# Batch 0's softmax denominators in two halves, output stores on SyncE's queue, and a re-planned order of work, in an attention-plus-feed-forward kernel

## The chip, the cores and the metric

One NeuronCore of a Trainium2 chip runs the whole kernel. The metric is device time in microseconds (us) of one execution; less is better. The kernel before was timed four times.

## What is computed

Inputs are q, k and v (8 batches, 8 heads, 576 positions, head size 64), `moe_w_in` (512 x 2048) and `moe_w_out` (2048 x 512), all float32. The reference, cut to what matters:

```python
q_d, k_d, v_d = means over groups of 4 neighbouring positions      # 144 of them
out_d  = softmax(q_d @ k_d.T / 8) @ v_d                            # coarse attention, 144 x 144
out_up = np.repeat(out_d, 4, axis=2)
s      = q @ k.T / 8, masked to |i - j| < 4
out_local = softmax(s) @ v                                         # a band of 7
x = (out_up + out_local), heads side by side                       # 4608 tokens x 512
h = x @ w_in
g = np.where(h > 0, h, exp(min(h, 0)) - 1)
out = g @ w_out                                                    # 4608 x 512
```

## The kernel before, in words

Heads are worked on in pairs: four pairs for each batch. The tokens of all batches stand in one row and are cut into nine blocks of 512 for the feed-forward part, so block 0 needs only batch 0, and block 1 needs batches 0 and 1.

All five engines work from one list, the string `ORDER`. A loop at the end of the kernel takes its words one by one and emits the instructions of each. Every engine executes its own instructions strictly in the order of the list and waits only for its operands and for its buffers, so the list is the schedule. The words, with b the batch, j the pair, t the token block and fc one of 16 slices of the hidden layer:

- `Lq Lk Lv b.j` load q, k or v of a pair by SyncE's queue (SP; lines 306 and 316), into ten staging buffers. `Dq Dk b.h` load two pairs of q or k at once, converted to 16 bits on the way, by GpSimd's queue (POOL; line 336). `WI0`-`WI3` and `WO0`-`WO3` load the weights, also by POOL (lines 266, 271). `WL` holds a staging buffer for a load.
- `Cq Ck Cv` convert to 16 bits on POOL (lines 354, 359).
- `Tq Tk` turn q and k by TensorE (PE), `Aq Ak` copy them out of PSUM (mostly ScalarE, ACT), `Fq Fk` sum fours on VectorE (DVE).
- `SL` and `SD` are the local and the coarse scores of a pair (PE), and `SC` is both together. `G0 G1` and `H0 H1` are their exponentials on ACT (lines 502, 508), and `E0 E1` are both together. `M` applies the mask on DVE.
- `VS` sums v in fours by PE (line 369), `VD` copies the sum out (DVE).
- `DEN` sums the exponentials of all four pairs of a batch into denominators (PE, line 539, 96 small matmuls), `RC` takes the reciprocal (DVE), `RB` spreads it to 128 rows (PE, line 573).
- `OUT` is probabilities times v (PE, lines 584 and 590), `LG` copies it out (ACT, lines 599 and 602), `MUL` multiplies by the reciprocals (DVE), `X b.j.t` adds the local and the coarse part into block t (mostly POOL, line 627).
- `mm1.t.fc` is a slice of x @ w_in (4 matmuls, PE, line 635); for block 0, `Q0`-`Q2` do the first three quarters of slices 0 to 3. `e`, `m` and `g` are the exponential (ACT, line 660), the minimum (DVE, line 664) and the sum (DVE, line 669) of the activation. `mm2.t.i` is a quarter of a 128-token row block of g @ w_out (4 matmuls, PE, line 679). `oc` copies the result out of PSUM (ACT, line 686), and `st` stores it (line 690).
- `Z1`-`Z3` put that many dummy matmuls ("busy", line 251) ahead of the next PE step that takes a fresh PSUM buffer of kind `two` or `more`.

PSUM buffers: `two` (2 buffers) for turns, v sums, outputs, spreads and later scores; `more` (2 buffers) for batch 0's scores, its denominators, its last v sum and the first two spreads. When `Q0` comes up, the room of `more` is handed to `hp` and `misc`, which hold the slices of mm1, the results of mm2 and later denominators.

A DMA on SP's or ACT's queue counts its landing on one of eight semaphores that both queues share. In the built program each of these DMAs waits for an earlier one that used its semaphore to land. The wait stands on the engine that issues the DMA. The stores are issued by ACT:

```python
def store(t, tt):                                      # L688
    r = TBLK * t + 128 * tt
    nc.scalar.dma_start(out=out[r : r + 128, :], in_=oss.pop((t, tt))[:])
```

and the denominators are one step:

```python
den = dens[b] = more("den")[:, 0, :] if b == 0 else bank("misc", "den")
...
                    for j in range(NPAIR):
...
                        nc.tensor.matmul(
                            den[32 * j : 32 * j + 32, 0:RG], lhsT, rhs,
...
                            tile_position=(0, 32 * j),
```

Of the kernel before, what the change touches and what calls it, by code (L numbers as in the profile page):

```python
# [27 lines left out]
NPAIR = H // 2  # L28
# [8 lines left out]
X_DVE, K_DVE = ((0, 3, 0),), ((0, 0), (0, 1))  # L37
ORDER = """
KM Lq0.0 KV TBL Lk0.0 FILL Lq0.1 KN Lk0.1 KE Lq0.2 KI Lk0.2 Cq0.0 Ck0.0 Lq0.3 Tq0.0 Lk0.3 Aq0.0
Tk0.0 Cq0.1 Lv0.0 Ak0.0 Ck0.1 Lv0.1 Z1 Tq0.1 Fq0.0 Lv0.2 SL0.0 Cq0.2 Aq0.1 Lv0.3 Fk0.0 Ck0.2  # L40
Tk0.1 G00.0 Z1 Tq0.2 Ak0.1 Cq0.3 G10.0 Fq0.1 Aq0.2 SD0.0 Ck0.3 Tk0.2 H00.0 Fk0.1 H10.0 KS Ak0.2
M0.0 SL0.1 Z2 Tq0.3 G00.1 Fq0.2 Cv0.0 G10.1 Fk0.2 Aq0.3 SD0.1 M0.1 Tk0.3 H00.1 H10.1 Fq0.3 Cv0.1
Ak0.3 SL0.2 Z1 VS0.0 Dq1.0 Fk0.3 G00.2 G10.2 VD0.0 WI0 SD0.2 WI1 Z2 VS0.1 H00.2 H10.2 Cv0.2
SL0.3 VD0.1 M0.2 G00.3 Z3 VS0.2 G10.3 Dk1.0 M0.3 SD0.3 OUT0.0 H00.3 VD0.2 WI2 H10.3 LG0.0 Z1
DEN0 WI3 WLv1.0 OUT0.1 Cv0.3 Lv1.0 RC0 Lv1.1 LG0.1 Lv1.2 VS0.3 RB0.0 Lv1.3 VD0.3 MUL0.0 RB0.1 Z1
OUT0.2 MUL0.1 X0.0.0 OUT0.3 LG0.2 X0.0.1 LG0.3 RB0.2 X0.1.1 X0.1.0 MUL0.2 Z1 RB0.3 Q0 MUL0.3
X0.2.1 X0.2.0 Q1 X0.3.0 Dk1.1 Q2 Dq1.1 mm1.0.0 mm1.0.2 e.0.0 X0.3.1 Tq1.1 WO0 Tk1.1 e.0.2 m.0.0
mm1.0.1 g.0.0 Ak1.1 WO1 mm1.0.3 Aq1.1 m.0.2 mm1.0.6 Fk1.1 WO2 e.0.3 Fq1.1 e.0.1 Tq1.0 Dk2.0
Tk1.0 Aq1.0 m.0.3 m.0.1 Ak1.0 g.0.1 WO3 SC1.1 Fq1.0 WLv2.0 Dq2.0 Lv2.0 mm1.0.7 Fk1.0 E01.1 Lv2.1
Cv1.0 Lv2.2 g.0.3 E11.1 Lv2.3 g.0.2 VS1.0 Lq3.0 mm1.0.11 VD1.0 e.0.7 M1.1 mm1.0.13 e.0.6 m.0.7  # L50
e.0.11 g.0.7 SC1.0 m.0.6 e.0.13 mm1.0.5 m.0.11 g.0.11 E01.0 m.0.13 mm1.0.9 E11.0 g.0.13 g.0.6
Tq1.2 Tk1.2 M1.0 Aq1.2 mm1.0.14 Ak1.2 Lk3.0 Cv1.1 Fq1.2 OUT1.0 e.0.5 Fk1.2 mm1.0.4 e.0.9 m.0.5
LG1.0 g.0.5 Tq1.3 e.0.4 Dq2.1 m.0.9 VS1.1 g.0.9 Aq1.3 mm2.0.0 VD1.1 e.0.14 Fq1.3 Tk1.3 OUT1.1
Ak1.3 Dk2.1 m.0.4 g.0.4 LG1.1 Fk1.3 SC1.2 m.0.14 g.0.14 mm2.0.1 E01.2 mm1.0.12 E11.2 mm1.0.8
e.0.12 M1.2 SC1.3 Lv3.0 m.0.12 e.0.8 g.0.12 Cv1.2 E01.3 m.0.8 mm1.0.10 g.0.8 E11.3 VS1.2 e.0.10
mm1.0.15 M1.3 VD1.2 DEN1 e.0.15 m.0.10 g.0.10 OUT1.2 m.0.15 mm2.0.2 RC1 LG1.2 g.0.15 RB1.1 RB1.0
MUL1.1 mm2.0.3 MUL1.0 X1.1.1 RB1.2 oc.0.0 MUL1.2 X1.0.2 mm2.0.4 X1.1.2 X1.0.1 Tq2.1 st.0.0 Tk2.1
Aq2.1 Cv1.3 mm2.0.5 Ak2.1 Fq2.1 X1.2.1 VS1.3 Fk2.1 Tq2.2 X1.2.2 mm2.0.6 Aq2.2 VD1.3 OUT1.3 Fq2.2
RB1.3 LG1.3 mm2.0.7 MUL1.3 Tk2.2 oc.0.1 mm2.0.8 Cv2.0 Lq3.1 Ak2.2 mm2.0.9 X1.3.2 Fk2.2 X1.3.1
mm2.0.10 st.0.1 Cv2.1 mm2.0.11 VS2.0 oc.0.2 mm2.0.12 Cv2.2 Lk3.1 VD2.0 SC2.1 mm2.0.13 E02.1  # L60
mm2.0.14 E12.1 Cv2.3 Lv3.1 mm2.0.15 M2.1 Tq2.0 oc.0.3 Cq3.0 Lq3.2 Tk2.0 Aq2.0 mm1.1.0 Ak2.0
Fq2.0 mm1.1.2 e.1.0 Ck3.0 Lk3.2 Fk2.0 SC2.2 e.1.2 m.1.0 g.1.0 E02.2 m.1.2 mm1.1.4 Lv3.2 g.1.2
Cv3.0 E12.2 Lq3.3 Tq2.3 e.1.4 M2.2 mm1.1.1 Aq2.3 Lk3.3 m.1.4 VS2.3 st.0.3 g.1.4 Cq3.1 Tk2.3
e.1.1 VD2.3 mm1.1.3 Ak2.3 m.1.1 Lv3.3 g.1.1 Ck3.1 SC2.0 e.1.3 Fk2.3 mm1.1.7 E02.0 m.1.3 g.1.3
E12.0 VS2.2 Fq2.3 Cv3.1 Lq4.0 mm1.1.5 e.1.7 VD2.2 M2.0 SC2.3 e.1.5 m.1.7 mm2.1.0 Lk4.0 E02.3
g.1.7 m.1.5 E12.3 mm1.1.6 g.1.5 Lv4.0 VS2.1 M2.3 e.1.6 mm1.1.8 VD2.1 m.1.6 DEN2 e.1.8 g.1.6
Cv3.2 Lq4.1 OUT2.1 RC2 mm1.1.9 LG2.1 m.1.8 g.1.8 RB2.1 st.0.2 OUT2.3 e.1.9 MUL2.1 mm1.1.10 LG2.3
m.1.9 RB2.3 g.1.9 X2.1.3 e.1.10 OUT2.0 X2.1.2 MUL2.3 mm1.1.11 LG2.0 m.1.10 RB2.0 g.1.10 X2.3.2
e.1.11 mm2.1.1 MUL2.0 Cv3.3 mm1.1.12 m.1.11 g.1.11 X2.0.3 OUT2.2 e.1.12 X2.0.2 RB2.2 LG2.2
mm1.1.14 m.1.12 g.1.12 X2.3.3 Tq3.0 e.1.14 MUL2.2 mm1.1.13 Aq3.0 Cq3.2 Tk3.0 m.1.14 e.1.13 Lk4.1  # L70
mm2.1.2 VD3.0 X2.2.2 Ak3.0 g.1.14 Tq3.2 Ck3.2 KD3.0 mm1.1.15 m.1.13 Aq3.2 Lv4.1 g.1.13 Cv4.0
Lq4.2 Tk3.2 e.1.15 VD3.2 X2.2.3 mm1.2.0 Ak3.2 m.1.15 g.1.15 Tq3.1 e.2.0 KD3.2 mm2.1.3 Aq3.1
Cq3.3 Tk3.1 m.2.0 oc.1.0 Lk4.2 mm1.2.2 VD3.1 Cq4.1 Ak3.1 g.2.0 Ck4.0 mm2.1.4 st.1.0 KD3.1 e.2.2
Ck3.3 SC3.1 mm1.2.12 m.2.2 E03.1 Lv4.2 g.2.2 Cv4.1 Lq4.3 mm2.1.5 E13.1 mm1.2.1 e.2.12 M3.1 SC3.0
m.2.12 e.2.1 g.2.12 mm2.1.6 E03.0 m.2.1 g.2.1 mm1.2.10 E13.0 Cv4.2 Tq3.3 e.2.10 Tk3.3 M3.0 Aq3.3
mm1.2.15 m.2.10 Ak3.3 g.2.10 Cq4.0 mm2.1.7 e.2.15 VD3.3 Lk4.3 KD3.3 mm2.1.8 m.2.15 oc.1.1 Lv4.3
g.2.15 st.1.1 SC3.3 Lq5.0 Lk5.0 mm2.1.9 E03.3 mm2.1.10 E13.3 mm1.2.5 M3.3 SC3.2 e.2.5 mm1.2.6
E03.2 m.2.5 g.2.5 mm2.1.11 E13.2 Tq4.0 e.2.6 M3.2 oc.1.2 Tk4.0 m.2.6 mm2.1.12 st.1.2 g.2.6 Ck4.2
Ak4.0 DEN3 Aq4.0 Ck4.1 KD4.0 mm2.1.13 VD4.0 Lv5.0 RC3 Lq5.1 mm2.1.14 SO3 mm2.1.15 Tq4.1 oc.1.3
Tk4.1 st.1.3 Cq4.2 mm1.2.3 Aq4.1 Cq5.0 Ak4.1 Lk5.1 mm1.2.7 VD4.1 Lv5.1 e.2.3 KD4.1 Tq4.2 Lq5.2  # L80
e.2.7 m.2.3 g.2.3 Tk4.2 SI3 Cq4.3 mm2.2.0 m.2.7 g.2.7 Ck4.3 Aq4.2 Lk5.2 mm1.2.9 Ak4.2 Ck5.0
VD4.2 Lv5.2 mm1.2.4 e.2.9 KD4.2 m.2.9 SC4.2 e.2.4 g.2.9 E04.2 m.2.4 mm1.2.11 g.2.4 E14.2
mm1.2.13 e.2.11 M4.2 SC4.1 e.2.13 m.2.11 mm2.2.1 g.2.11 E04.1 m.2.13 mm1.2.8 E14.1 g.2.13
mm1.2.14 e.2.8 M4.1 m.2.8 SC4.0 e.2.14 g.2.8 E04.0 m.2.14 mm2.2.2 g.2.14 E14.0 OUT3.0 mm2.2.3
MUL3.0 Cv4.3 OUT3.1 oc.2.0 M4.0 Lq5.3 OUT3.3 st.2.0 Lk5.3 MUL3.1 X3.0.3 mm2.2.4 Lv5.3 X3.0.4
MUL3.3 mm2.2.5 X3.1.3 mm2.2.6 X3.3.4 X3.1.4 OUT3.2 X3.3.3 Tq4.3 MUL3.2 Cv5.1 mm2.2.7 Aq4.3
X3.2.3 Tk4.3 VD4.3 oc.2.1 mm2.2.8 Ck5.2 Ak4.3 mm1.3.0 st.2.1 X3.2.4 KD4.3 Cv5.0 SC4.3 e.3.0
mm1.3.3 Cv5.2 E04.3 Lq6.0 m.3.0 mm2.2.9 E14.3 g.3.0 Tq5.0 e.3.3 M4.3 mm1.3.7 Aq5.0 m.3.3 g.3.3
Cq5.1 DEN4 e.3.7 VD5.0 Cq5.3 Lk6.0 mm1.3.6 RC4 m.3.7 Tk5.0 SO4 g.3.7 Tq5.1 e.3.6 Ck5.1 Ak5.0
mm1.3.5 m.3.6 Aq5.1 Lv6.0 g.3.6 Cq5.2 mm2.2.10 Lq6.1 e.3.5 KD5.0 VD5.1 Lk6.1 mm1.3.1 m.3.5 Lv6.1  # L90
g.3.5 Lq6.2 Tk5.1 e.3.1 mm1.3.8 Lk6.2 Ak5.1 m.3.1 g.3.1 mm2.2.11 SI4 KD5.1 mm1.3.11 e.3.8 SC5.1
oc.2.2 m.3.8 g.3.8 e.3.11 mm2.2.12 E05.1 m.3.11 g.3.11 mm1.3.10 E15.1 mm1.3.9 e.3.10 M5.1 st.2.2
SC5.0 m.3.10 e.3.9 mm2.2.13 g.3.10 E05.0 m.3.9 mm1.3.13 g.3.9 E15.0 mm1.3.4 e.3.13 M5.0 Tq5.2
m.3.13 e.3.4 g.3.13 Tk5.2 Aq5.2 mm2.2.14 m.3.4 g.3.4 Ck5.3 Ak5.2 mm1.3.2 VD5.2 Ck6.0 Lv6.2 KD5.2
mm2.2.15 e.3.2 m.3.2 OUT4.2 oc.2.3 g.3.2 OUT4.0 st.2.3 MUL4.2 mm1.3.14 Cv5.3 mm2.3.0 MUL4.0
e.3.14 X4.2.4 Lq6.3 X4.2.5 OUT4.1 OUT4.3 m.3.14 MUL4.1 X4.0.5 mm2.3.1 X4.0.4 MUL4.3 mm1.3.12
X4.1.5 g.3.14 Tq5.3 e.3.12 X4.3.4 Tk5.3 X4.1.4 Aq5.3 mm1.3.15 m.3.12 Ak5.3 g.3.12 Cq6.1 mm2.3.2
e.3.15 VD5.3 X4.3.5 KD5.3 mm1.4.0 m.3.15 g.3.15 Ck6.2 SC5.3 e.4.0 Cq6.2 mm1.4.5 E05.3 m.4.0
mm2.3.3 E15.3 g.4.0 Cv6.1 mm2.3.4 e.4.5 Cv6.0 oc.3.0 Tq6.1 M5.3 st.3.0 mm1.4.9 m.4.5 Aq6.1 g.4.5
Cq6.0 mm2.3.5 VD6.1 e.4.9 Cv6.2 Lk6.3 mm1.4.1 Lv6.3 m.4.9 g.4.9 Lq7.0 SC5.2 e.4.1 Lk7.0 mm1.4.7  # L100
E05.2 m.4.1 g.4.1 mm2.3.6 E15.2 Tq6.0 e.4.7 M5.2 mm1.4.8 Aq6.0 m.4.7 g.4.7 DEN5 e.4.8 VD6.0
m.4.8 mm1.4.6 RC5 g.4.8 Tq6.2 SO5 e.4.6 Tk6.0 Cq6.3 Aq6.2 mm1.4.2 Ak6.0 m.4.6 mm2.3.7 g.4.6
Cq7.0 e.4.2 KD6.0 Ck6.1 mm1.4.15 VD6.2 oc.3.1 st.3.1 m.4.2 mm2.3.8 Lv7.0 e.4.15 g.4.2 Lq7.1 SI5
m.4.15 mm2.3.9 Lk7.1 g.4.15 Lv7.1 Tk6.1 Lq7.2 mm1.4.3 Ak6.1 Tk6.2 KD6.1 e.4.3 mm2.3.10 Ck7.0
Lk7.2 Ak6.2 mm1.4.11 m.4.3 g.4.3 Ck6.3 mm2.3.11 KD6.2 e.4.11 Lv7.2 m.4.11 SC6.1 oc.3.2 g.4.11
mm1.4.12 E06.1 mm2.4.0 E16.1 mm1.4.4 e.4.12 M6.1 SC6.0 m.4.12 e.4.4 g.4.12 mm2.3.12 st.3.2 m.4.4
E06.0 g.4.4 mm1.4.13 E16.0 mm2.4.1 e.4.13 M6.0 OUT5.3 m.4.13 OUT5.2 MUL5.3 mm1.4.10 MUL5.2
mm2.3.13 X5.3.6 e.4.10 g.4.13 X5.3.5 mm2.3.14 X5.2.5 m.4.10 mm2.3.15 g.4.10 X5.2.6 OUT5.1 oc.3.3
# [76 lines left out]
def kernel(  # L185
# [92 lines left out]
    def nines(b):  # L278
        return b in NINES
# [481 lines left out]
```

The softmax here doesn't subtract the row's maximum and nothing guards it: scores larger than these inputs give would overflow.

## Time and profile before

| what | before |
|---|---|
| median of 4 runs (lowest, highest) | 366.91 us (366.32, 367.44) |
| the profiled execution: its own time, and the span of its instructions | 366.4 us, 364.6 us |
| PE busy | 347.7 us, 95% of the span |
| DVE, ACT, POOL busy | 66%, 57%, 33% |
| first matmul of mm1 (`Q0`) starts | 27.65 us |
| last matmul ends (the last output copy starts) | 361.0 us |

Times in the profile count from the start of the span. A row of the timeline gives the start, the time it took, the engine, the line, the operation and its operands, how many instructions were merged into the row, and in brackets the engine's idle time before it with what ended it. "ACTq" and "SPq" are the instruction queues of the engines, in which a DMA is issued; the time of such a row is what the issuing engine spent on it. PE counts as busy in the dummy matmuls too. PEld is PE's weight load. A row of waits gives who waited for what, the total in us, how often, and the longest.

### The profile page before, as it was taken

How to read it: one execution, taken by the hardware profiler on the slowest of the kernel's cores; microseconds unless marked ns; L12 is line 12 of the kernel's file. 1: busy time of each engine (PE TensorE's matmuls, PEld its weight loads, DVE VectorE, ACT ScalarE, POOL GpSimd, SP SyncE). 2: the span in 40 equal slices, each digit the busy share in tenths (PEclk: the TensorE clock that was granted, in tenths of full speed). 3: DMA queues.
4: the chain of work that ended last, by engine and by line, in shares of the span. 5: the costliest groups of instructions: out<-in, count | busy, mean ns of one | idle time of the engine just before them, and what ended most of it. 6: DMA issues, size and time to landing. Idle time of an engine off the chain costs nothing.

```text
span 364.6 us, 9507 instructions
## 1 busy us (share of the span) xinstructions
PE 347.7 (95%) x3953; PEld 182.2 (50%) x3953; DVE 240.6 (66%) x472; ACT 208.1 (57%) x395; POOL 120.3 (33%) x177
## 2 busy tenths in 40 slices
PE   7878989899999999999999999999999999999995
PEld 3654454445565564554555545555544444444442
DVE  2857986449897548587896677878564755455520
ACT  2845882478678759477566665776454334344321
POOL 6768224450374141860472319311400410000000
PEclk9999999999999999999999999999999999999999
DMA  8999999999869779399659842022014110010012
GB/s 273 201 200 200 198 196 198 210 176 192 160 135 211 128 168 179 82 217 171 147 108 199 194 85 69 30 80 64 31 33 111 44 45 30 29 59 29 29 59 86
DMA packets 106917, 46.08 MB, mean 126 GB/s; under 512 B 92314, under 2 KB 101178, under 8 KB 106874
## 3 DMA queue, kind: packets, MB, share of 16 engines
q1 hardware_dynamic: 91402, 25.17, 40.3%
q10 hardware_dynamic: 8896, 13.36, 12.7%
q0 software_dynamic: 6576, 6.94, 11.1%
q8 instruction: 31, 0.51, 0.6%
q14 instruction: 12, 0.10, 0.1%
HBM read 42.49 MB, written 9.53 MB: 143 GB/s over the span
## 4 chain that ended last, share of the span: by engine, by line
PE 77%; DMA 7%; DVE 4%; ACT 3%; issue 3%; POOL 2%; SPq 2%; ACTq 1%; POOLq 0%
PE op L679 32%; PE hp L635 29%; DMA v<-in_v_dram 6%; PE lg L584 3%; PE sc L476 2%; DVE gt L669 2%; PE den L539 2%; SPq L316 2%; PE tq L369 2%; PE tq L392 2%; PE tk L392 1%; DVE e L664 1%; DMA q<-in_q_dram 1%; ACT e L660 1%; PE lg L590 1%
## 5 line engine op out<-in xcount | busy, mean ns | idle before, releaser
L635 PE MATMUL hp<-xt,WI 128*128 128x512 f16 x576 | 142.8, 379 | 2.5 <-DVE gt L669 2.3
L679 PE MATMUL op<-WO,gt 128*128 128x512 f16 x576 | 139.8, 380 | 0.4 <-DVE gt L669 0.3
L660 ACT ACTIVATE e<-hp 128x512 f16<-128x512 f32 x144 | 85.7, 601 | 75.5 <-PE hp L635 69.9
L669 DVE SCALAR_TENSOR_TENSOR gt<-hp,e 128x512 f16<-128x512 f32 x144 | 99.2, 690 | 4.7
L679 PEld LDWEIGHTS <-gt 128*128 128x128 f16 x576 | 53.2, 98 | 62.0 <-DVE gt L669 1.6
L664 DVE TENSOR_SCALAR e<-e 128x512 f16<-128x512 f16 x144 | 52.4, 365 | 48.1 <-ACT e L660 47.1
L635 PEld LDWEIGHTS <-WI 128*128 128x128 f16 x576 | 53.1, 97 | 61.7 <-issue 4.7
L627 POOL TENSOR_TENSOR xt<-ln,gn 128x64 f16<-128x64 f16 (+7 forms) x63 | 41.7, 683 | 64.9 <-DVE ln L614 64.6
L502 ACT ACTIVATE pex<-sc 112x576 f16<-112x576 f32 x64 | 41.0, 647 | 5.5 <-PE sc L486 4.2
L686 ACT COPY os<-op 128x512 f32<-128x512 f32 x36 | 21.1, 586 | 40.1 <-PE op L679 37.1
L359 POOL CAST v<-v 112x768 f16<-112x768 f32 x30 | 24.6, 830 | 41.8 <-PE lg L584 22.6
L521 DVE TENSOR_TENSOR mex<-pex,MASK 112x1152 f16<-112x1152 f16 x32 | 25.4, 793 | 13.0 <-ACT pex L502 12.9
L354 POOL CAST q<-q 96x768 f16<-96x768 f32 x20 | 16.8, 840 | 31.0 <-issue 21.2
L354 POOL CAST k<-k 96x768 f16<-96x768 f32 x20 | 17.3, 873 | 27.1 <-PE tk L392 20.6
L508 ACT ACTIVATE dex<-sc 72x288 f16<-72x288 f32 x64 | 25.4, 404 | 1.3 <-PE sc L486 1.3
L417 ACT CAST qt<-tq 128x720 f16<-128x720 f32 x20 | 15.2, 760 | 11.4 <-PE tq L369 7.9
L476 PEld LDWEIGHTS <-kt 64*112 64x112 f16 x384 | 13.1, 127 | 14.0 <-issue 10.0
L476 PE MATMUL sc<-qt,kt 64*112 64x96 f16 x384 | 16.9, 217 | 2.1 <-ACT kt L412 0.6
L369 PEld LDWEIGHTS <-VR 112*72 112x72 f16 x192 | 12.9, 113 | 6.9 <-ACT qt L412 2.8
L614 DVE TENSOR_TENSOR ln<-lg,rcb 128x576 f16<-128x576 f32 x20 | 15.0, 748 | 0.0
L450 DVE CAST vd<-tq 72x256 f16<-72x256 f32 x20 | 8.3, 415 | 8.7 <-ACT qt L417 8.6
L584 PEld LDWEIGHTS <-v 112*64 112x64 f16 x384 | 10.2, 109 | 7.4 <-issue 5.3
(64 smaller groups left out, 272.4 us busy)
## 6 DMA issues: line engine op xcount, KB each, us to landing
v<-in_v_dram SPq DMA_DIRECT2D x28, 336.0 KB, 7.5
out_dram<-os ACTq DMA_DIRECT2D x36, 256.0 KB, 2.7
q<-in_q_dram SPq DMA_DIRECT2D x24, 288.0 KB, 5.4
k<-in_k_dram SPq DMA_DIRECT2D x24, 288.0 KB, 6.7
rcb<-rd ACTq DMA_DIRECT2D x10, 360.0 KB, 5.5
WI<-in_moe_w_in_dram POOLq DMA_DIRECT2D x4, 512.0 KB, 10.8
WO<-in_moe_w_out_dram POOLq DMA_DIRECT2D x4, 512.0 KB, 15.5
q<-in_q_dram POOLq DMA_DIRECT2D x4, 288.0 KB, 10.5
```

Source lines behind the costliest of these rows:

```text
L354: nc.gpsimd.tensor_copy(out=t, in_=x.rearrange("p (e c d) -> p c e d", e=2, d=D))
L359: nc.gpsimd.tensor_copy(out=t[:], in_=st32.pop(("v", b, j)).rearrange("p (e c) d -> p c e d", e=2))
L476: nc.tensor.matmul(sc[e][0:KW, c // 3, QB * (c % 3) : QB * (c % 3) + QB], kt[r, QB * c : QB * c + KW], q_of(b, j, r, c), start=True, stop= ...
L502: nc.scalar.activation(out=stS[(b, j)][2][:, e, :].rearrange("p (g u) -> p g u", g=2), in_=scs[(b, j)][e][0:KW, :, 0:HB], func=AF.Exp, sca ...
L508: nc.scalar.activation(out=stS[(b, j)][1][:, e], in_=scs[(b, j)][e][0:KG, :, HB : HB + SD], func=AF.Exp, scale=SCALE / 16.0,)
L521: nc.vector.tensor_tensor(out=mex[:], in0=pex[:], in1=mk2, op=AB.mult)
L627: eng.tensor_tensor(out=xts[t][:, j, t0 - TBLK * t : t1 - TBLK * t], in0=ln[:, a:z], in1=_rep4(gn[:, a // 4 : z // 4]), op=AB.add,)
L635: nc.tensor.matmul(hps[(t, fc)][:], WI[:, dc, 128 * fc : 128 * fc + 128], xts[t][:, dc, :], start=(dc == 0), stop=(dc == DMC - 1),)
L660: nc.scalar.activation(out=e[:], in_=hps[(t, fc)][:], func=AF.Exp)
L664: nc.vector.tensor_scalar(out=e[:], in0=e[:], scalar1=1.0, scalar2=-1.0, op0=AB.min, op1=AB.add)
L669: nc.vector.scalar_tensor_tensor(out=gts[t][:, fc, :], in0=hps[(t, fc)][:], scalar=0.0, op0=AB.max, in1=els.pop((t, fc))[:], op1=AB.add,)
L679: nc.tensor.matmul(ops[(t, tt)][:], gts[t][:, fc, 128 * tt : 128 * tt + 128], WO[:, fc, :], start=(fc == 0), stop=(fc == FCN - 1),)
```

## The change

There are three parts.

1. **Denominators.** `den_mm` takes an optional half. `DH0.0` sums pairs 0 and 1 of batch 0 and `DH0.1` pairs 2 and 3 (48 matmuls each, into different PSUM buffers). `half_recip` (`RH`) takes the reciprocal of 64 rows. The first half stands after `SD0.2`, ahead of the scores of pair 3. Only `RB0.2` still uses a `more` buffer.
2. **Stores.** `store` issues on `nc.sync` in place of `nc.scalar`.
3. **The list.** All of `ORDER` is planned anew. Its steps are the same apart from `DEN0 RC0`, which became `DH RH`, and the dummy matmuls: PE has 7 matmuls more before Q0.

The diff also brings a second way to get v's sums of four (`V4`, with words `U` and `V`); `V4` is empty, so it emits nothing, apart from a constant `IND` twice as wide (112 x 104).

```diff
+V4, STORE_SP = (), True
+RB_MORE = ((0, 2),)
...
-    ind = np.zeros((KW, 52), dtype=np.float16)
+    ind = np.zeros((KW, 104), dtype=np.float16)
...
-    def den_mm(b):
-        den = dens[b] = more("den")[:, 0, :] if b == 0 else bank("misc", "den")
+    def den_mm(b, half=None):
+        pairs = range(NPAIR)
+        if half is None:
+            den = dens[b] = bank("misc", "den")
+        else:
+            pairs = pairs[2 * half : 2 * half + 2]
+            den = dens[(b, half)] = (more if half else two)("den")[:, 0, :]
...
-                    for j in range(NPAIR):
+                    for j in pairs:
...
+    def half_recip(b, half):
+        if half == 0:
+            stR[b] = sb.tile([128, RG], FP16, tag="rc", bufs=2, name="rc")
+        r = slice(64 * half, 64 * half + 64)
+        nc.vector.reciprocal(out=stR[b][r], in_=dens[(b, half)][r, 0:RG])
...
-        rb, rc = (more if b == 0 and j < 2 else two)("rb"), stR[b]
+        rb, rc = (more if (b, j) in RB_MORE else two)("rb"), stR[b]
...
-        nc.scalar.dma_start(out=out[r : r + 128, :], in_=oss.pop((t, tt))[:])
+        eng = nc.sync if STORE_SP else nc.scalar
+        eng.dma_start(out=out[r : r + 128, :], in_=oss.pop((t, tt))[:])
```

The list where batch 0 ends, before:

```
M0.0 SL0.1 Z2 Tq0.3 G00.1 Fq0.2 Cv0.0 G10.1 Fk0.2 Aq0.3 SD0.1 M0.1 Tk0.3 H00.1 H10.1 Fq0.3 Cv0.1
Ak0.3 SL0.2 Z1 VS0.0 Dq1.0 Fk0.3 G00.2 G10.2 VD0.0 WI0 SD0.2 WI1 Z2 VS0.1 H00.2 H10.2 Cv0.2
SL0.3 VD0.1 M0.2 G00.3 Z3 VS0.2 G10.3 Dk1.0 M0.3 SD0.3 OUT0.0 H00.3 VD0.2 WI2 H10.3 LG0.0 Z1
DEN0 WI3 WLv1.0 OUT0.1 Cv0.3 Lv1.0 RC0 Lv1.1 LG0.1 Lv1.2 VS0.3 RB0.0 Lv1.3 VD0.3 MUL0.0 RB0.1 Z1
OUT0.2 MUL0.1 X0.0.0 OUT0.3 LG0.2 X0.0.1 LG0.3 RB0.2 X0.1.1 X0.1.0 MUL0.2 Z1 RB0.3 Q0 MUL0.3
```

and after:

```
SL0.1 Z3 Tq0.3 Fq0.2 G00.1 Cv0.0 Lv0.3 G10.1 Fk0.2 Z3 VS0.0 Aq0.3 M0.1 Fq0.3 SD0.1 Tk0.3 Cv0.1
H00.1 H10.1 Dq1.0 Ak0.3 SL0.2 Fk0.3 WI0 G00.2 G10.2 VD0.0 Dk1.0 Z2 VS0.1 M0.2 Cv0.2 SD0.2 VD0.1
DH0.0 H00.2 H10.2 WI1 VS0.2 RH0.0 WI2 SL0.3 VD0.2 Z2 OUT0.0 G00.3 WI3 G10.3 RB0.0 WLv1.0 LG0.0
Lv1.0 M0.3 SD0.3 Lv1.1 H00.3 Cv0.3 Lv1.2 MUL0.0 OUT0.1 H10.3 Z1 DH0.1 LG0.1 X0.0.1 X0.0.0 VS0.3
RH0.1 RB0.1 VD0.3 Z2 OUT0.2 MUL0.1 Z1 RB0.2 LG0.2 X0.1.0 OUT0.3 MUL0.2 Z2 RB0.3 LG0.3 X0.1.1 Q0
```

The list around the first store, before:

```
MUL1.1 mm2.0.3 MUL1.0 X1.1.1 RB1.2 oc.0.0 MUL1.2 X1.0.2 mm2.0.4 X1.1.2 X1.0.1 Tq2.1 st.0.0 Tk2.1
Aq2.1 Cv1.3 mm2.0.5 Ak2.1 Fq2.1 X1.2.1 VS1.3 Fk2.1 Tq2.2 X1.2.2 mm2.0.6 Aq2.2 VD1.3 OUT1.3 Fq2.2
```

and after:

```
mm1.0.10 Fk2.1 DEN1 e.0.10 m.0.10 SC2.1 g.0.10 E02.1 RC1 mm2.0.2 E12.1 RB1.2 mm2.0.3 MUL1.2
Cv1.3 Lv2.2 RB1.1 oc.0.0 M2.1 VS1.3 st.0.0 mm2.0.4 MUL1.1 X1.2.2 X1.2.1 mm2.0.5 VD1.3 X1.1.2
```

SP's own sequence becomes, after the loads of batch 1: `Lv2.0 Lv2.1 Lv2.2 st.0.0 Lv2.3 Lq3.0 st.0.1 Lk3.0 Lv3.0 Lq3.1 Lk3.1 st.0.2 Lv3.1 ...`. In the built program `st.0.0` shares its semaphore with `Lv0.3`; before, it shared it with `Lv2.1`.

## The prediction

> **What bounds the kernel now.** I read the strips of the page first, then busy times by stretch, then PE's blocks of work one after the other in the timeline, and last the waits.
>
> ```profile
> PE   7878989899999999999999999999999999999995
> DVE  2857986449897548587896677878564755455520
> ACT  2845882478678759477566665776454334344321
> DMA  8999999999869779399659842022014110010012
> ```
>
> A slice is 9.1 us. PE is full from slice 10 on; only the first 90 us have holes, and there the DMA engines are full too. So what the change can win lies ahead of 90 us.
>
> ```profile
> 36.00:54.00 18.00, 16.10 (x212) 8.47 (x210) 16.17 (x32) 15.19 (x33) 4.55 (x7) 1.00 1.21 197
> 54.00:66.00 12.00, 9.51 (x226) 5.54 (x227) 7.31 (x16) 4.38 (x9) 5.39 (x8) 1.00 1.21 196
> 95.00:200.00 105.00, 104.05 (x1272) 57.56 (x1270) 78.80 (x155) 70.76 (x134) 46.80 (x62) 1.00 0.86 158
> ```
>
> The columns are the stretch, then busy us of PE, PEld, DVE, ACT and POOL, the granted clock, the DMA share and GB/s. From 36 to 54 DVE and ACT are busy 16.2 and 15.2 of 18 us, so they pace PE. From 54 to 66 nothing is full but the DMA, and PE loses 2.5 us: something waits there.
>
> To size this I took from the timeline the time from the start of each PE block to the start of the next where nothing waits: a group of four mm1 or mm2 matmuls 0.86 us (0.96 ahead of a smaller shape), `SC` 0.57, `OUT` 0.50, `DEN` 0.90, `RB` 0.42, `VS` 0.35, a turn 0.31 to 0.40 (batches 3 to 7: q 0.65, k 0.32). Summed over the list from Q0 to the end this gives 321.6 us before. Q0 starts at 27.65 and PE ends at 361.0, so waits take about 11.5 us: 4.0 up to `VS1.2` at 54.02 (DVE and ACT mostly), 2.9 from there to `OUT1.3` at 67.15, 1.75 up to 91, and 2.85 afterwards, 0.44 of it at 349.57, where the last groups wait for `g`. The large item is this:
>
> ```profile
> 59.73 0.59 ACT L686 COPY os<-op 128x512 f32<-128x512 f32 x1 [1.75 <-PE op L679]
> ...
> 62.22 0.81 POOL L359 CAST v<-v 112x768 f16<-112x768 f32 x1
> ...
> 64.13 0.38 ACTq L690 DMA_DIRECT2D out_dram<-os  x1
> ...
> 64.55 0.64 ACT L412 CAST qt<-tq 128x576 f16<-128x576 f32 x1 [4.23 <-DMA v<-in_v_dram]
> ...
> 65.24 0.53 PE L369 MATMUL vs<-v,VR 112*72 112x128 f16 x6 [2.30 <-ACT qt L412]
> ```
>
> The output was copied by 60.32, but ACT issued its store only at 64.13. It waited for a load of v: the store shares a completion semaphore with `Lv2.1`, issued at 51.44 and landed at 64.05. Behind the store on ACT stood the copy `Aq2.1`, which frees the PSUM buffer for `VS1.3`; PE stood still for 2.30 us.
>
> **The stores.** Moved to SP, `st.0.0` shares its semaphore with `Lv0.3`, landed by 20.20 before, so ACT no longer stands. The next latest for `VS1.3` is the cast `Cv1.3`, 62.22 to 63.03, which in the new list is ahead of POOL's `X1` work. So 65.24 falls to 63.1: about -2.2 us, and 0.2 less behind it. A rule speaks against any gain. The Trainium skill, DMA: Bandwidth & Descriptors, section "Issuing engines are not separate DMA queues", says that issuing from another engine saves only the issuer's own time, which is small beside the transfer. By the rule 36 stores at 0.34 to 0.38 us free 13 us of an ACT that is 57% busy, worth 0 on PE's path. By the row it is 2.2, since the engine also carries the wait. I take the row.
>
> What it costs: SP now waits for `oc`, with loads queued behind. `st.0.0` holds `Lv2.3` until about 63.2 (before: issued at 60.85, landed at 67.49), so it lands near 70; its cast is due near 75. `st.0.1` holds `Lk3.0` until about 70 (before 64.49); with the 7 us from issue to landing of that time it lands at 77, cast due near 79, and PE needs it only 20 us later. Cost 0, and 1 to 2 us if that slack is gone. The stores' own landing behind queued loads (7 us, not 4.4) is covered by two `os` buffers, used some 14 us apart. At the end SP replaces ACT as issuer of the last store: within 0.1 us.
>
> **The denominators.** The gain sought is an earlier Q0. These are the rows:
>
> ```profile
> 18.20 0.89 POOL L359 CAST v<-v 112x768 f16<-112x768 f32 x1
> ...
> 19.15 0.49 PE L369 MATMUL vs<-v,VR 112*72 112x128 f16 x6 [0.67 <-POOL v L359]
> ...
> 22.23 0.28 PE L539 MATMUL den<-dex,IND 72*32 72x72 f16 x10 [0.64 <-issue]
> ...
> 22.54 0.61 DVE L547 RECIPROCAL rc<-den 128x72 f16<-128x72 f32 x1 [2.44 <-PE den L539]
> ```
>
> Taken off the path: `DEN0` took 20.69 to 22.51, of which 0.64 is an issue gap. A half is 48 matmuls in two column groups where `DEN0` had 96 in four. The trace shows no such half: it takes between 0.45 (half of 0.90) and 0.90 (the same steps, fewer side by side). I take 0.85, near the row. `DH0.0` falls before 19.15, where PE ran three dummy matmuls and waited 0.67 for the cast of v: hidden, or +0.85 without that cover. Of the issue gap, the Trainium skill (Runtime: NRT & Kernel Launch, section "Instruction fetch mechanics") says that fetch is mostly hidden, which would make the spreading of the list worth 0. The row has 0.64 on the path, and the new list puts 48 and not 96 of these in one place. I count it as gone, inside the chain below.
>
> But the new list also puts `SL0.3` behind `VS0.2`; before it started at 17.21, ahead of it. `VS0.2` waits for `Cv0.2`, and POOL has again three DMA issues (`Dq1.0 WI0 Dk1.0`) ahead of this cast, so it ends at 19.09 again. From there, with durations of the rows: `VS0.2` 19.15, `SL0.3` 19.55 to 20.05, its two exponentials (1.19) to 21.3, `LG0.0` (0.82) to 22.1, `H0.3` (0.70) to 22.75, a dummy and `DH0.1` to 23.8, `RH` (0.61) to 24.45, `RB0.1` (0.48) to 24.95. Then two dummies and `OUT0.2` to 25.85, `LG0.2` to 26.75, `MUL0.2` (0.97) to 27.75. `RB0.2` holds a `more` buffer until then, and Q0 needs that room. Q0 starts at 27.8, not 27.65. What the split gives, the order takes back: +0.15, between -1.5 (cast of v ready in time) and +1.0 (one more wait).
>
> **The list from Q0 on.** The same blocks in the new order sum to 321.3: -0.3, from fewer changes of shape. Up to `VS1.2` the new list has 21.9 us of PE work, the old 22.4. Two limits set when it starts. Its load `Lv1.2` landed at 52.88, because SP's queue moved only some 39 KB/us (192 KB in 45 to 50 us) as long as POOL's loads ran, and those are the same; with the cast that is 53.8. DVE: the list ahead of `VS1.2` holds 14 `m` (0.30), 14 `g` (0.66), 8 `F` (0.74), 4 `M` (0.76), 2 `VD` (0.42) and a `MUL` (1.0): 24.2 us, before one `M` fewer, 23.5. Before, 23.5 us took 26.4 from Q0 on, 89%. At 89% 24.2 take 27.2, so 55.0. ACT has 24.7 us against 23.4, and the same holds for it. I take 54.5 between the two limits: waits 4.8, before 4.0. From `VS1.2` to `OUT1.3` I put 0.5, before 2.9, the store's wait being gone. From there to 91, mm1 of block 1 is now mixed with the rest of mm2 of block 0, so DVE has 4 to 5 us for each 6.5 of PE, where before a stretch had 7.5 in 6.2: waits 0.9, before 1.75. After 91 I keep the same, less the 0.44: after the last mm1 three groups of mm2 now cover `e`, `m` and `g` (2.6 us against 1.9), before two (1.73).
>
> **The sum.** Waits 4.8 + 0.5 + 0.9 + 2.4 = 8.6, before 11.5: -2.9. With -0.3 and +0.15 it is -3.05. A new order has waits of its own that this trace cannot show: 0 to 2.85 (what the old list has after 91), and I take 0.65. That is -2.4 us. The profiled execution took 366.4 us, 1.8 around its span of 364.6, so it would become 364.0; it lies 0.5 under the median, and from the median I get 364.5.
>
> **The rivals.** (a) Likeliest, 50%: as above, 364.5, own range 363.6 to 365.6. (b) 15%: the casts of v come early enough that Q0 starts near 26.2 as well, and loads don't take it back: 362.8. For it: PE has slack ahead of 19. Against it: the DMA was full, and `Lv1.2` at 52.88 ends any lead. (c) 18%: the store's wait goes, but another takes its place (`Cv1.3` behind its load, or a load held behind a store): -0.3, 366.6. (d) 17%, slower: the stage from Q0 to `VS1.2`, with all four score blocks of batch 1 and 15 mm1 slices in it, makes DVE and ACT wait for each other. If DVE reaches 79% there and not 89%, its 24.2 us take 30.6 and `VS1.2` comes at 58.4, which is 3.9 over my sum: 368.4. From 80% down this outweighs the store. Against it: before, the same mix ran at 89%.
>
> **How the numbers follow.** About 0.3% (1.1 us) is what a measurement tells from no change: faster is below 365.8, slower above 368.0. Nearly all of (a) and (b) is faster, (c) is the same, (d) slower. The range runs from (b)'s value to between (c) and (d): 362.6 to 367.3.
>
> **What would show it.** In the profile after: no wait of ACT for a load of v ahead of a copy `qt`, and stores on SPq (right), or that wait again (wrong). Q0 between 26.8 and 28.8. `VS0.2` still released by the cast of v, and `SL0.3` after 19. `VS1.2` at 53.8 to 55.5. POOL casts of batch 3 that don't wait for loads. Wrong altogether if PE's idle time between 30 and 60 us grows by over 3 us, or if new waits appear behind 95 us.

## The result, and the profile after

The changed kernel takes 363.94 us (median of 43 runs, 360.65 to 367.6), the kernel before beside it 366.67 us (64 runs): ratio 0.9918, 95% interval 0.9902 to 0.9933, so 3.0 us less. Ratios, and the counts of half clock further down, leave out executions that took over 1.5% longer than the fastest of their kernel (of the changed one 6 of 44), while the medians are of all runs. The forecast was 364.5 us, 2.4 less. The profiled execution took 365.62 us with a span of 363.8: 1.7 over the median of its kernel and only 0.8 under the profiled one of before. Its trace should therefore hold something that costs time and that the median execution has less of. It shows in the strips of the page:

```profile
PE   7999987999999999999999999999999999999995
PEclk9999998799999999999999999999999999999999
DMA  8999999489997999757952399940023010010012
```

PE is full from 64 us on, not only from about 90; but in the seventh and eighth slice (55 to 73 us) the granted clock falls to 0.8 and 0.7, and in the eighth the DMA engines stand half idle. Before, the clock strip was 9 throughout. The same three stretches as before, in the view of busy times by stretch (us of PE, PEld, DVE, ACT, POOL, then granted clock, DMA share, GB/s):

```profile
36.00:54.00 18.00, 16.27 (x248) 8.77 (x249) 16.60 (x34) 16.53 (x36) 4.39 (x7) 1.00 1.21 197
54.00:66.00 12.00, 10.11 (x195) 5.04 (x194) 6.93 (x13) 4.41 (x10) 1.25 (x2) 0.79 0.96 156
95.00:200.00 105.00, 104.70 (x1210) 57.46 (x1211) 78.56 (x158) 70.73 (x135) 46.48 (x61) 1.00 0.83 146
```

From 54 to 66 PE had lost 2.5 us before. It now loses 1.9, and runs at 0.79 of its clock: fewer matmuls in the same time. PE's timeline names the place:

```profile
57.33 0.81 PE L681 MATMUL hp<-xt,WI 128*128 128x512 f16 x3
58.07 0.44 PE L573 MATMUL den<-mex,IND 112*32 112x72 f16 x32
...
58.97 0.45 PE L504 MATMUL sc<-qt,kt 64*112 64x96 f16 x9
61.31 0.33 PE L504 MATMUL sc<-qt,kt 64*112 64x96 f16 x3 [1.89 <-issue]
61.44 0.44 PE L514 MATMUL sc<-qt,kd 64*72 64x144 f16 x4
61.82 1.89 PE L725 MATMUL op<-WO,gt 128*128 128x512 f16 x4
63.63 0.78 PE L613 MATMUL rb<-rc,SEL 32*128 32x72 f16 x10
```

In the middle of `SC2.1`, after 9 of 12 matmuls of one form, PE stands for 1.89 us, and the releaser is "issue": no engine and no DMA of the kernel's data. Then four mm2 matmuls take 1.89 us where four took 1.04: half clock, granted from 61.06 to 67.89 by the trace.

Summed as in the prediction (time from block to block, less the block's own time without waits):

| us | before | predicted | after | den1_early (below) |
|---|---|---|---|---|
| `Q0` starts | 27.65 | 27.8 | 28.31 | 27.54 |
| waits up to `VS1.2` | 4.0 | 4.8 | 3.4 | 4.2 |
| `VS1.2` to `OUT1.3` | 2.9 | 0.5 | 5.2 | 1.5 |
| `OUT1.3` to 91 us | 1.7 | 0.9 | 0.2 | 0.3 |
| after 91 us | 2.9 | 2.4, and 0.65 for the new order | 1.7 | 1.7 |
| sum of the waits | 11.5 | 9.25 | 10.5 | 7.7 |

The store's wait is gone, as foreseen: SP issues it, and ACT has its output copied late only because PE was late.

```profile
66.27 0.59 ACT L732 COPY os<-op 128x512 f32<-128x512 f32 x1 [2.52 <-PE op L725]
...
66.88 0.37 SPq L737 DMA_DIRECT2D out_dram<-os  x1
```

In its place in the table stand 1.9 us of the stall and some 3 us of half clock, which no step of the prediction had.

### The profile page after: what moved, and what is told of

Read it like the earlier page. It is cut to its first block, busy times and chain, and to the rows that moved or that the text cites. A ratio compares the mean times of both kernels' runs of the same rounds, so it can differ in the third digit from the quotient of the medians.

```text
span 363.8 us, 9565 instructions
## 1 busy us (share of the span) xinstructions
PE 351.7 (97%) x3960; PEld 185.1 (51%) x3960; DVE 239.2 (66%) x473; ACT 208.9 (57%) x395; POOL 121.3 (33%) x177
## 4 chain that ended last, share of the span: by engine, by line
PE 83%; DMA 11%; POOL 2%; SPq 1%; issue 1%; ACT 1%; DVE 1%; ACTq 0%
PE op L725 35%; PE hp L681 31%; DMA v<-in_v_dram 10%; PE sc L504 3%; PE lg L624 2%; PE tq L391 2%; PE tq L414 2%; PE den L573 2%; PE tk L414 2%; SPq L319 1%; PE rb L613 1%; DMA MASK<-MASKc 1%; PE lg L630 1%; PE sc L514 1%; POOL WI L269 1%; PE vs L391 1%
## 5 line engine op out<-in xcount | busy, mean ns | idle before, releaser
L681 PE MATMUL hp<-xt,WI 128*128 128x512 f16 x576 | 144.3, 379 | 0.2
L725 PE MATMUL op<-WO,gt 128*128 128x512 f16 x576 | 142.7, 383 | 0.0
L710 DVE TENSOR_SCALAR e<-e 128x512 f16<-128x512 f16 x144 | 49.5, 344 | 51.6 <-ACT e L706 50.4
L376 POOL CAST q<-q 96x768 f16<-96x768 f32 x20 | 17.9, 899 | 20.4 <-issue 14.8
L624 PE MATMUL lg<-mex,v 112*64 112x96 f16 x384 | 13.7, 208 | 0.6 <-ACT lg L648 0.3
```

Source lines behind the costliest of these rows:

```text
L376: nc.gpsimd.tensor_copy(out=t, in_=x.rearrange("p (e c d) -> p c e d", e=2, d=D))
L624: nc.tensor.matmul(lg[64 * e : 64 * e + 64, c // 3, QB * (c % 3) : QB * (c % 3) + QB], v16[:, c, e, :], mex[:, e, QB * c : QB * c + QB], s ...
L681: nc.tensor.matmul(hps[(t, fc)][:], WI[:, dc, 128 * fc : 128 * fc + 128], xts[t][:, dc, :], start=(dc == 0), stop=(dc == DMC - 1),)
L710: nc.vector.tensor_scalar(out=e[:], in0=e[:], scalar1=1.0, scalar2=-1.0, op0=AB.min, op1=AB.add)
L725: nc.tensor.matmul(ops[(t, tt)][:], gts[t][:, fc, 128 * tt : 128 * tt + 128], WO[:, fc, :], start=(fc == 0), stop=(fc == FCN - 1),)
```

## The experiments

The theory on record, A: the large item is the wait of the store. B: the gain comes from the new order, with stores on either engine. C is drawn from the profile after: PE ran out of instructions at `SC2.1`. All kernels ran beside the kernel before; ratios are to it.

**stores_only.** The list of before, and one line:

```diff
-        nc.scalar.dma_start(out=out[r : r + 128, :], ...)
+        nc.sync.dma_start(out=out[r : r + 128, :], ...)
```

> The kernel before with its 36 stores issued by SP, the order of the list untouched. Theory A (on record: the store's wait was the large item): ACT no longer stands 4.23 us ahead of the copy qt at 64.55 and VS1.3 starts near 63.1 and not 65.24, so the time falls by 1.5 to 2.4 us (364.3 to 365.2). Theory B (the gain comes from the new order, the old one has other waits behind the store): within 0.7 us of before, with a wait of the same size on the load or the cast of v at VS1.3, or later on a load of batch 3 that was held behind a store on SP.

Measured: ratio 0.998 (0.9957 to 0.9998), 0.8 us. ACT copies `qt` at 63.53 without waiting for a load, and `VS1.3` no longer waits for that copy:

```profile
65.07 0.49 PE L368 MATMUL vs<-v,VR 112*72 112x128 f16 x6 [0.15 <-POOL v L358]
```

Yet it starts at 65.07 (before 65.24): in this execution the time was lost earlier, at `VS1.0`. First POOL, then PE:

```profile
36.77 0.70 POOL L335 DMA_DIRECT2D q<-in_q_dram  x1 [1.04 <-DMA WI<-in_moe_w_in_dram]
37.46 0.83 POOL L358 CAST v<-held 112x768 f16<-112x768 f32 x1
```

```profile
38.35 0.49 PE L368 MATMUL vs<-v,VR 112*72 112x128 f16 x6 [1.92 <-POOL v L358]
38.68 3.53 PE L634 MATMUL hp<-xt,WI 128*128 128x512 f16 x8
```

POOL's DMA issue waited for the load of the last slice of `WI` (landed at 36.48, before at 35.28), the cast of v stood behind it, and PE waited 1.92 us for the cast. Then it ran at half clock (eight mm1 matmuls in 3.53 us). From `VS1.2` to `OUT1.3` PE now takes 10.5 us, where it took 13.1 with the wait, but it came to `VS1.2` at 56.33 and not at 54.02. A is right on the mechanism and wrong on the size.

**store_later.** The list of before with `st.0.0`, still on ACT, moved behind the copies that stood behind it:

```diff
-Tq2.1 st.0.0 Tk2.1 Aq2.1 Cv1.3 mm2.0.5 Ak2.1 Fq2.1
+Tq2.1 Tk2.1 Aq2.1 Cv1.3 mm2.0.5 Ak2.1 st.0.0 Fq2.1
```

> The kernel before with one word moved: st.0.0, still issued by ACT, stands behind the copies Aq2.1 and Ak2.1 and not ahead of them. If what the store costs is only what stands behind its wait, this gives what SP gave in the same list (stores_only: ratio 0.998), within 0.5 us of it (365.3 to 366.3), and VS1.3 is no longer released by a copy qt. If the issuing itself on ACT (36 times 0.38 us) cost something, this stays at the time of before. On record I had 2.2 us for it; stores_only says that a part comes back as other waits ahead of VS1.3.

Measured: 0.997 (0.9939 to 1.0002), the same as stores_only within the intervals, and by itself just not clear of no change. PE's wait at `VS1.3` is 0.15 us, where it was 2.30:

```profile
64.75 0.49 PE L368 MATMUL vs<-v,VR 112*72 112x128 f16 x6 [0.15 <-POOL v L358]
```

Here too `VS1.2` to `OUT1.3` takes 10.5 us. So the engine that issues makes no difference that shows in the list of before; what stands behind the wait does.

**act_stores.** The changed kernel with `STORE_SP = False`.

> The changed kernel with its stores issued by ACT again, the new order kept. Theory A: ACT stands again for a load of v ahead of the first store, and PE waits 2 us for a copy behind it: 2 us slower than the changed kernel (about 366). Theory B: as fast as the changed kernel within 0.7 us (363.2 to 364.7), since in the new order st.0.0 comes some 9 us after the issue of the load whose semaphore it would share, or because PE is behind anyway by its own stall at 59.4.

Measured: 0.996 (0.9941 to 0.9984), 1.6 us slower than the changed kernel with intervals that do not meet: nearer to the 2 us of A than to the 0.7 of B. Its trace, of an execution of 362.50 us without half clock, speaks for B all the same:

```profile
63.43 0.59 ACT L731 COPY os<-op 128x512 f32<-128x512 f32 x1 [0.70 <-PE op L724]
64.92 0.41 ACTq L736 DMA_DIRECT2D out_dram<-os  x1
66.97 0.64 ACT L644 COPY lg<-lg 128x576 f32<-128x576 f32 x1 [2.96 <-PE lg L629]
```

The store again waits, until `Lv2.2` lands at 64.84, but in the new order nothing behind it is due: ACT's next copy waits for PE anyway, and `VS1.3` comes on time (63.75). Where the 1.6 us are lost, this trace does not show.

**new_head, old_head.** Heads exchanged at `Q0`: new_head is the changed head with the list of before and stores by ACT, old_head the head of before with the new list and stores by SP.

```
 new_head:  ORDER = head(after) + ["Lv1.3"] + list(before)
 old_head:  ORDER = head(before) + list(after) without "Lv1.3"
```

> The head of the changed kernel (up to Q0, denominators of batch 0 in two halves, 13 fillers) with the list of before from Q0 on and stores by ACT. My sum on record: the halves give nothing, Q0 starts 0.2 to 0.7 us later (28.3 in the changed kernel, 27.65 before), time the same as before within 0.7 us. Rival: the halves are the gain: 1.5 us or more faster than before.

> The head of before (denominators of batch 0 in one piece) with the new list from Q0 on and stores by SP; it undoes the halves alone. My sum on record: the halves give nothing, so this takes what the changed kernel takes, within 0.7 us (363.2 to 364.7), Q0 at 27.5 to 27.8 against 28.3. Rival: the halves are needed, 1.5 us or more slower than the changed kernel.

Measured: new_head 1.001 (0.9986 to 1.0032), old_head 0.991 (0.9888 to 0.9941). The halves are worth nothing that can be measured (the intervals leave room for about 1 us), in either list; what is gained comes behind `Q0`.

**den1_spread.** `DEN1` in two lots of 48 matmuls into the same buffer, one mm1 group between them:

```diff
-LG1.2 m.0.12 g.0.12 mm1.0.10 Fk2.1 DEN1 e.0.10
+LG1.2 m.0.12 g.0.12 DP1.0 mm1.0.10 Fk2.1 DP1.1 e.0.10
```

> The changed kernel with DEN1 issued as two lots of 48 matmuls, the first ahead of mm1.0.10, the second behind it. Theory C (in the changed kernel PE stood 1.89 us after DEN1 because it used up its instructions faster than the next 256 came, and the stall in turn was followed by two windows of half clock, 61.3 to 67.9): the gap at SC2.1 is gone, 1.9 us for the gap and up to 3 us for the clock: 359.5 to 362, and granted clock 1.0 in nearly all executions. Rival: the next 256 instructions come late whatever stands in front, so the gap moves behind the second lot or to the next block: within 0.7 us of the changed kernel. Second rival: the gap goes and half clock stays: about 362.

Measured: 0.992 (0.9892 to 0.9952), as the changed kernel. C in this form falls: the gap stays.

```profile
58.92 0.45 PE L574 MATMUL den<-mex,IND 112*32 112x72 f16 x32
59.19 0.31 PE L574 MATMUL den<-dex,IND 72*32 72x72 f16 x16
59.42 0.45 PE L503 MATMUL sc<-qt,kt 64*112 64x96 f16 x9
61.68 0.25 PE L503 MATMUL sc<-qt,kt 64*112 64x96 f16 x3 [1.80 <-issue]
```

But it comes after the same 9 matmuls. That is the clue: a fixed count of instructions. The page lists transfers of the kind "instruction" (queue, count, MB, share):

```profile
q8 instruction: 31, 0.51, 0.6%
```

That is 16 KB each. PE has 7,920 matmuls and weight loads, so a transfer holds 256 instructions of 64 bytes. old_head confirms the count: its head has seven dummy matmuls less, 14 instructions with their weight loads, and there the gap stands 14 instructions later, ahead of the first mm2 matmul:

```profile
59.64 0.51 PE L475 MATMUL sc<-qt,kt 64*112 64x96 f16 x12
59.98 0.29 PE L485 MATMUL sc<-qt,kd 64*72 64x144 f16 x4
62.35 1.62 PE L678 MATMUL op<-WO,gt 128*128 128x512 f16 x4 [2.08 <-issue]
```

Counted from the start of the trace, the gap stands behind PE's record 1,985 in all seven traces that show one of over 0.7 us here (the changed kernel, act_stores, den1_spread, old_head, and below den1_early, early_act and head_fix), whatever instruction stands there. And the 0.64 us gap in `DEN0` of the kernel before, a term of the prediction, stands behind record 705, which is 5 times 256 earlier.

So C, mended: when PE enters one lot of 256, the next is called for, and PE must not be through before it is there. In the changed kernel PE enters in `OUT1.2` at 55.7; the transfer is seen in the DMA from 58.61 to 59.70; PE goes on at 61.31, after 5.6 us. Its own work on the 256 is 3.7 us, since `DEN1` alone is 192 of them in 0.90 us. In the list of before the same lot held mm2 groups (8 instructions in 0.86 us) and lasted 9.5 us, 2.3 of them the store's wait.

A lot can be shorter than that where the DMA is not full. The one with `DEN3` in it, in the same trace, lasts 3.38 us and PE is busy through all of it and on behind it:

```profile
129.44:132.82 3.38, 3.38 (x131) 2.67 (x130) 2.73 (x8) 2.24 (x5) 2.13 (x3) 1.00 0.56 148
```

The DMA share is 0.56 there, and the next lot's transfer ran from 129.42 to 130.33, as soon as PE entered; from 55.7 to 61.3 the share is 1.22, as in every full stretch, and the transfer began 2.9 us after the entry.

**den1_early.** One word of the list moved, so that half of `DEN1` falls into the lot ahead:

```diff
-g.0.11 VS1.2 e.0.12 ... mm1.0.10 Fk2.1 DEN1 e.0.10
+g.0.11 DEN1 VS1.2 e.0.12 ... mm1.0.10 Fk2.1 e.0.10
```

> The changed kernel with one word of the list moved: DEN1 stands ahead of VS1.2 and not behind mm1.0.10. Theory C, mended after den1_spread (the gap came at the same instruction, after 9 or 10 of the 12 matmuls of SC2.1, wherever the 192 instructions of DEN1 stood in front of it; from the crossing 256 instructions earlier, in OUT1.2 at 55.7, it took 2.9 us until the fetch was seen in the DMA, 1.1 for it, and 1.6 more until PE went on, 5.6 in all, while PE's own work on these 256 is only 3.6 us): now about half of DEN1 lies ahead of the crossing, the 256 last about 5 us, and the gap shrinks from 1.89 to between 0 and 0.7 us. Time 1.2 to 2 us under the changed kernel (362 to 362.7), more if half clock gets rarer too. Rival: the gap stays near 1.9 us at the same instruction, so it has nothing to do with how fast instructions are used up: within 0.7 us of the changed kernel.

Measured: 361.93 us, 0.986 (0.9822 to 0.9905); the interval just touches that of the changed kernel, which begins at 0.9902.

```profile
59.15 0.45 PE L503 MATMUL sc<-qt,kt 64*112 64x96 f16 x9
60.54 0.25 PE L503 MATMUL sc<-qt,kt 64*112 64x96 f16 x3 [0.94 <-issue]
```

The gap is 0.94, a little more than expected, because 6.5 us pass here from PE's entry into the lot to its going on. None of its six executions ran a window at half clock, where 23 of 38 of the changed kernel did. Those of the changed kernel that ran none have a median of 362.5 us, so by these medians some 0.6 of the 2.0 us that den1_early gains are the gap, and the rest is half clock that stays away.

**early_act.** den1_early with the stores on ACT.

> den1_early (DEN1 ahead of VS1.2) with the stores issued by ACT: what SP as issuer is worth where the stall of PE is small. In act_stores ACT's wait for a load ended at 64.9 with nothing due behind it and PE lost nothing by it, so the store's wait is gone by the new order alone: within 0.7 us of den1_early (361.3 to 362.7). If ACT's 36 issues or its wait do cost: 1 us or more above den1_early.

Measured: 0.986 (0.9827 to 0.9894), as den1_early. Where the stall is small, no gain from SP as issuer shows. But with six executions each, the two intervals leave room for 2 us either way, so this does not refute the 1.6 us of act_stores.

**best.** den1_early with two mm2 groups ahead of `SC2.1`, and `RC1` earlier on DVE for the buffer that they need:

```diff
-mm1.0.10 Fk2.1 e.0.10 m.0.10 SC2.1 g.0.10 E02.1 RC1 mm2.0.2
+mm1.0.10 Fk2.1 e.0.10 m.0.10 mm2.0.4 mm2.0.5 SC2.1 g.0.10 E02.1 mm2.0.2
```

> den1_early with mm2.0.4 and mm2.0.5 moved ahead of SC2.1 (and RC1 behind VD1.2), so that the 256 instructions up to the middle of SC2.1 last 1.7 us longer. Theory C: the gap of 0.94 us at SC2.1 in den1_early goes to 0, time 0.5 to 1 us under den1_early (361 to 361.5). Rival: the fetch comes later still, or DVE makes mm2.0.4 wait: no gain or a loss.

Measured: 362.06 us (six executions, one of them 371.63 at a granted clock of 0.971), 0.985 (0.9809 to 0.9885); its interval lies below that of the changed kernel (0.9902 to 0.9933), but is not separated from den1_early. The gap is gone:

```profile
59.64 1.89 PE L724 MATMUL op<-WO,gt 128*128 128x512 f16 x8
61.46 0.51 PE L503 MATMUL sc<-qt,kt 64*112 64x96 f16 x12
61.81 0.29 PE L513 MATMUL sc<-qt,kd 64*72 64x144 f16 x4
```

`RB1.0` now waits 0.83 us for DVE, so most of the last 0.94 comes back at once; C's further 0.5 to 1 us is not shown.

**head_fix, both.** The changed kernel with `SL0.3` ahead of `VS0.2` and `VD0.1` ahead of `M0.2`; "both" adds the edit of den1_early.

> The changed kernel with two words of its head moved: SL0.3 ahead of VS0.2, and VD0.1 ahead of M0.2, since in the changed kernel VS0.2 and SL0.3 waited 0.57 us for a buffer that VD0.1 frees, and VD0.1 stood behind the 1.37 us of M0.2 on DVE. If the order takes back what the halves give (as on record), Q0 comes 0.5 to 1.2 us earlier (27.1 to 27.8). The time: 0.5 to 1.0 us less if the stage behind is paced by the engines, within 0.5 us if loads of v pace it (Lv1.2 landed at 52.6 in every list so far).

> Both edits together. Theory C and an earlier Q0: 361.5 to 362.5. If loads of v pace the stage before 54 us: as den1_early alone, within 0.5 us.

Measured: head_fix 0.994 (0.9913 to 0.9965), `Q0` at 28.32; both 0.988 (0.9836 to 0.992), `Q0` at 28.06. A miss: `Q0` came no earlier. In head_fix `VS0.1` waited 0.87 us for the cast of v instead, and the gap at `SC2.1` was 2.27 us. `Q0` also came at 27.65 and 27.08 in two executions of the kernel before, so single traces do not settle half a microsecond of the head.

**before_again.** The kernel before, unchanged, for a second trace.

> The kernel before, unchanged, for a second trace of it. In 107 executions of it that ran beside the others its time hardly depended on how long the clock was halved (366.5 with one window of 3.4 us, 366.5 with two), where the changed kernel's rose by 1.5 us a window. If the wait for Lv2.1 takes up what half clock costs ahead of it: VS1.3 at 65 to 66 whatever the sum of waits ahead of it, and released by ACT's copy qt.

Measured: 368.64 us in one run, clock 0.990.

```profile
64.81 0.53 PE L369 MATMUL vs<-v,VR 112*72 112x128 f16 x6 [2.70 <-ACT qt L412]
...
65.76 1.42 PE L679 MATMUL op<-WO,gt 128*128 128x512 f16 x4
```

PE came to the store's wait 0.8 us earlier than in the first trace (62.12 against 62.94) and stood 2.70 us and not 2.30; in new_head, which has the same wait, it came at 63.85 and stood 1.76. Half clock here came behind the wait (66.28 to 73.11), not ahead of it, so the expectation that the wait hides half clock was not tested by this trace.

## Why the prediction was right, point by point

The time and the sign were right; the sum came out through errors against each other, so part of the agreement is luck: the store's term was too large and the stall was missed, while the gain late in the list was put too small.

- **The wait of the store.** Right that it goes. Its term, 2.2 us, was too large for the typical execution: taken away alone it gave 0.8 us (stores_only) and 1.1 (store_later, whose interval reaches zero). The three traces of this wait say why, in part: the load `Lv2.1` landed at 63.63, 64.05 and 64.43, so `VS1.3` started at 64.81, 65.24 and 65.62 although PE was ready over a range of 1.7 us. What PE had lost ahead of it was taken up by the wait, and comes through when the wait is gone: in the two traces without it PE reached `VS1.2` 2.0 to 2.3 us later than in the first of before and started `OUT1.3` only 0.3 to 0.6 us earlier. I took the full wait of one execution. That what PE lost ahead of the wait is half clock in most executions was not shown.
- **The rule on issuing engines** was weighed rightly against the row in this: what counted was not the 36 issues but what stood behind one wait. In the list of before SP was not needed for it: store_later does as much on ACT. In the new list the traces of act_stores and early_act show no wait of PE behind a store on ACT; yet act_stores is 1.6 us slower than the changed kernel, and that stays open.
- **The issue gap.** This step failed. I counted the 0.64 us at `DEN0` as gone, and it is; but the new order made a larger one of the same kind, 1.89 us at `SC2.1`, and I looked for one only where the diff spreads the list. The Trainium skill (Runtime: NRT & Kernel Launch, section "Instruction fetch mechanics") calls the fetch mostly hidden. Behind `DEN3`, at a DMA share of 0.56, it is; where the DMA engines are full, 256 instructions took 5.0 to 6.5 us to come, and 192 of them can be used up in 0.90 us. There the measurement decides.
- **The head.** Right that the split gives nothing: new_head and old_head both say so. `Q0` at 28.31 lies in the range given (26.8 to 28.8). The cause that I named is wrong: `VS0.2` was not released by the cast of v but by a buffer, which `VD0.1` frees behind the 1.37 us of `M0.2` on DVE:

```profile
17.74 1.37 DVE L549 TENSOR_TENSOR mex<-pex,MASK 112x1152 f16<-112x1152 f16 x1
...
19.04 0.41 DVE L478 CAST vd<-vs 72x256 f16<-72x256 f32 x1
...
19.50 0.53 PE L391 MATMUL vs<-v,VR 112*72 112x128 f16 x6 [0.57 <-DVE vd L478]
```

- **A half of the denominators**, 48 matmuls in two column groups: `DH0.0` began at 17.97 and ended at 18.94, 0.97 us. I had 0.85, near the upper bound; from start to end, the 96 of `DEN1` took 0.97 as well (58.07 to 59.04), so a half is no shorter than the whole.
- **The stage up to `VS1.2`.** `VS1.2` at 53.54, a little under the 53.8 to 55.5 given; waits 3.4 us and not 4.8. Rival (d) did not come: DVE was 92% busy from 36 to 54, and not 79%, as was ACT.
- **The stage behind `OUT1.3`.** My gain here was too small by half: waits fell from 4.6 to 1.9 us, where I had 3.3 and 0.65 for the unknown. No PE gap of over 0.15 us is left after 70 us. This is the main gain, and it is the new order's: in the nine traces with the new list these waits are 1.3 to 3.2 us, in stores_only, store_later and new_head, with the old one, 3.6 to 3.9. Which part of the new order does it, no run separates. The 0.65 us put aside for waits that the new order brings was too little in another place.
- **Loads held behind stores on SP.** Casts of batch 3 do wait for loads (4.11 us at 88.53, 3.58 at 92.93), against what I listed; they cost PE nothing, as I had priced it.
- **Two slips in my sums.** 361.0 less 27.65 less 321.6 is 11.75, not 11.5; the forecast uses differences of the terms and does not change by it. And in rival (d) DVE at 83%, not 80%, would already take back the 2.4 us of the store.
- **The 0.8 of the profiled execution against the 3.0.** Half clock can be counted for every execution, in windows of 3.4 us, from its mean granted clock. The changed kernel took 362.5 us with no window (15 executions), 364.1 with one (14) and 365.5 with two (9); the profiled one had two. The profiled execution of before, from which I forecast, had none, which is rare: for the kernel before, 122 executions show 365.4 with none (5), and 366.6, 366.4 and 366.7 with one, two and three. The difference goes with the head of the kernel more than with its list behind `Q0`: with the old head and the new list, old_head took 363.3, 363.8 and 364.0 with one, two and three; with the new head and the old list, new_head took 365.9, 368.1 and 368.9 with none, one and two. (store_later, with head and list of before, does rise, 364.0, 366.5 and 367.0 with one, two and three, in nine executions.) The old head also ran without a window far more rarely (5 of 122 and 1 of 18, against 15 of 38 and 12 of 22). That its windows lie in the head and cost little there would fit, and two traces have such windows (below), but it is not shown. Why the changed kernel beats act_stores (0.9918 against 0.9962), while den1_early does not visibly beat early_act, stays open too.

## What to carry to other kernels

A list of instructions has a second budget beside time: count PE's instructions with their weight loads in lots of 256, and where the DMA is full, see that each lot lasts longer than its fetch takes, here 5.0 to 6.5 us; a block of many tiny matmuls should straddle a boundary or share its lot with large ones. A wait that ends with a transfer landing at its own time takes up what was lost ahead of it: its length in one good execution is an upper bound of what its removal gives. And if a wait is costly for what stands behind it, try moving the one instruction down its own list: here that gave as much as another engine did.

## What the runs showed of the hardware

Behind `Q0`, half clock follows a gap of PE. Nine gaps of 1.75 to 2.70 us occur in the fourteen traces; after seven of them the clock was halved, beginning between 0.3 us ahead of the gap's end and 2.0 us behind it, for 3.41 or 6.83 us. Two (1.76 us in new_head, 2.30 in the first trace of before) were not followed; nor was any gap of 1.65 us or less. In the head it came without such a gap too, in two traces with the head of before, whose PE has fewer matmuls there: old_head (25.09 to 31.92) and store_later (two windows ahead of 21.2). The Trainium skill (TensorE: Matmul & The Clock Gate, Part 1) has this gate, with a free-running window of 3.4 us; the lengths agree, and a free-running window would explain that a gap of the same length is followed by half clock only in some cases, which no run here tests. But it asks for an idle window, and here gaps of 1.8 to 2.7 us, half to four fifths of one, were followed by half clock.

The fetch of 256 instructions, in seven traces, from the entry of PE into the lot ahead to its going on: 5.6 us (changed kernel), 5.0 (act_stores), 5.7 (den1_spread), 5.8 (old_head), 6.0 (head_fix), 6.3 (early_act), 6.5 (den1_early). Of this about 0.9 to 1.4 is the transfer as the DMA's records show it, and always 1.5 to 1.8 us pass from its end to PE's next matmul.
